# Two ends of a one-core transformer block: the opening dummy matmuls as products of zeros, and the last output block in two column halves

## The chip, the cores and the metric

The kernel runs on one core of one Trainium2 chip. The metric is the device time of one execution in microseconds (us), given as the median of several runs. Five engines take part: TensorE (PE in the profile; its weight loads are a track of their own, PEld), VectorE (DVE), ScalarE (ACT), GpSimd (POOL) and SyncE (SP), which here issues all DMA transfers.

## The reference, cut to what matters

```python
# attention: 2 x 8 heads, 768 tokens, head size 64
q_bits = (q @ proj > 0); k_bits = (k @ proj > 0)          # 6 bits each, a bucket number
scores = where(q_bucket == k_bucket, q @ k.T / 8, -1e9)
a = softmax(scores) @ v                                    # -> x, 2 x 768 x 512
# token and channel mixing
theta = x @ w_theta
u = x + w_tok_r @ (x * cos(theta)) + w_tok_i @ (x * sin(theta))
u = u + relu(u @ w_ch)
# the last layer: 512 -> 2048 -> 512
out = u + relu(layer_norm(u) * g_ln @ w_ch1) @ w_ch2       # 1536 rows of 512 columns
```

## The kernel before, in words

All operands are 32-bit floats. Most matrix products are made of three TensorE instructions each: an operand is split into a rounded high part (`hi`, `hh`, ...) and a remainder (`lo`, `hl`, ...), and high x high, high x low and low x high are added up in PSUM. The order of instructions on every engine is written out by hand: the strings of operation names (`head`, `tail`, `half1`, `trans`, `odd`, `even`, `last`) are walked through from left to right, and each engine executes its own instructions in that order.

**The opening.** Six loads are issued on SP: the first head pair's keys in two halves, the first quarter of the projection (`pbr`), the queries in two halves, and a small table. GpSimd writes a 128x128 identity (`make_identity`), a constant, zeros into `pb_lo` (512 columns), and zeros into two key tiles. `warm(16)` is placed last before the string `head`: it issues 16 TensorE transpositions of the identity into PSUM bank T0, whose result nobody reads. They keep TensorE at work while the first loads are on their way. The string `head` then starts with the splitting of keys and queries (`sh` on ScalarE, `sl` on VectorE), the splitting of the projection (`pb`: `pb_hi` by ScalarE and VectorE, the left 64 columns of `pb_lo` by ScalarE), and the first products: `ac.0` to `ac.3` (the bits of half the keys, the other half, half the queries, the other half; two matmuls of 384 columns each, line 286; `ac.0` writes into the same bank T0 as the dummies), `D.0.0` and `D.0.1` (the first two row blocks of scores, six matmuls each, line 503), `Q.0.0` and `Q.0.1` (the bucket terms added to them, line 515), and `warm.17`, 17 more transpositions of the identity. On VectorE the order is `lok` for two halves, `loq` for two halves (lines 221, 101), four comparisons `bb` (line 310), and the row maxima `M` (line 340); on ScalarE the exponentials `E` (line 356) follow the maxima.

**The end.** The last layer runs in rounds: a round takes 256 of the 2048 hidden columns (a group `g`) and half of the rows (768, six blocks of 128). `o_mm(r, t)` makes the second product of round `r` for row block `t`: six matmuls of 512 output columns into one PSUM bank (T0 and O in turn). `o_add(r, t)` adds the bank to the row block's running sum `U` on VectorE, and in the last group stores the finished block with one DMA of 128 rows of 2 KB. After the last round five such blocks follow each other; block 5 is the last work of the kernel.

Of the kernel before, what the change touches and what calls it, by code (L numbers as in the profile page):

```python
# [9 lines left out]
F32 = mybir.dt.float32  # L10
# [23 lines left out]
def attn_moe_kernel(  # L34
# [28 lines left out]
    vec, act, pool, pe, sp = nc.vector, nc.scalar, nc.gpsimd, nc.tensor, nc.sync  # L63

    def f(ap):
        return ap.bitcast(F32)

    const = ctx.enter_context(tc.tile_pool(name="const", bufs=1))
    psum = ctx.enter_context(tc.tile_pool(name="psum", bufs=1, space=PSUM))

    def bank(tag, name):
        return psum.tile([128, 512], F32, tag=tag, name=name)
# [77 lines left out]
    pb_lo = bp.tile([128, NP, 128], F32R, name="pb_lo")  # L150
# [4 lines left out]
    def r_new(j, dt, name):  # L155
        return const.tile([128, 2, 512], dt, tag=f"R{j}", name=name)
# [4 lines left out]
    def load_raw(n, place=None, which=(0, 1)):  # L161
        b, j = divmod(n, NP)
        for x in which:
            nm, src = (("k", kT), ("q", qT))[x]
            t = place[:, x, :] if place is not None else raw_new(nm, n)
            sp.dma_start(out=t, in_=src[b, 2 * j:2 * j + 2].rearrange("e d s -> (e d) s"))
            raw[nm, n] = t
# [322 lines left out]
    def warm(n):  # L490
        ps = bank("T0", "warm")
        for x in range(n):
            pe.transpose(ps[:, 0:128], ident, ident)  # L493
# [48 lines left out]
    sp.dma_start(out=cst_sb, in_=cst)  # L542
    load_raw(1)
    sp.dma_start(out=pbr[:, 1:NP], in_=pb[:, 1:NP])
    make_identity(nc, ident)
    pool.memset(halfpi, math.pi / 2)
    pool.memset(f(pb_lo), 0.0)
    for t in kz:
        pool.memset(f(t[64:128]), 0.0)
    warm(16)  # L550
    TS = tuple(range(22, 46, 3))
    bg, bg2, bg3 = {}, {}, {}

# [29 lines left out]
    for i in range(8):  # L583
        c, x = divmod(i, 2)
# [74 lines left out]
    def bp_(x, e):  # L659
# [21 lines left out]
        n=s_norm, U=p_transpose, H=p_hi, L=p_lo, PV=pv_mm, O=pv_evac_a, X=pv_evac_b,  # L681
# [48 lines left out]
    def U(i):  # L730
        if i not in U_AT:
            return U0[:, i if i < 4 else i - 2, :]
        j, y = U_AT[i]
        if j not in ur:
            ur[j] = r_new(j, F32, f"u{j}")
        return ur[j][:, y, :]
# [251 lines left out]
    W1, W2 = {}, {}  # L988
# [135 lines left out]
    h_t, ps_t, sn_t, c_t, o_t = {}, {}, {}, {}, {}  # L1124
# [44 lines left out]
        hh, hlo = h_t[r, c]  # L1169
        vec.scalar_tensor_tensor(out=hlo, in0=c_t.pop((r, c)), scalar=0.0, in1=f(hh), op0=ALU.max, op1=ALU.subtract)  # L1170

    def o_mm(r, t):
        g, s = rounds[r]
        e, i = divmod(t, TB)
        ps = o_t[r, t] = bank(("T0", "O")[t % 2], f"o{r}{t}")
        k = 0
        for x in range(2):
            hh, hlo = h_t[r, 10 * (x + 1) + e + 1]
            for lt, y in ((hh, 0), (hh, 1), (hlo, 0)):
                pe.matmul(ps, lt[:, i * 128:(i + 1) * 128], W2[g][:, y, x, :], start=(k == 0), stop=(k == 5))  # L1180
                k += 1

    def o_add(r, t):
        g, s = rounds[r]
        c = ORD[6 * s + t]
        u = U(c)
        vec.tensor_tensor(out=u, in0=o_t.pop((r, t)), in1=u, op=ALU.add)  # L1187
        if g == NG - 1:
            sp.dma_start(out=out[c * 128:(c + 1) * 128, :], in_=u)


    ops.update(
# [2 lines left out]
        ch_br=ch_br, ch_bs=ch_bs, ln_a=ln_a, ln_b=ln_b, ln_c=ln_c, xb_new=xb_new, xn=xn_make, xb_t=xb_t, xb_e=xb_e,  # L1195
        xb_a=xb_a, xb_h=xb_h, xb_l=xb_l, ld=cv_ld, cv_y=cv_y, cv_s=cv_s, cv_b=cv_b, cv_p=cv_p, cv_j=cv_j, cv_h=cv_h, cv_l=cv_l, w1_s=w1_s,
        w1_h=w1_h, w1_l=w1_l, prod=prod, snap=snap, h_add=h_add, h_hi=h_hi, h_lo=h_lo, o_mm=o_mm, o_add=o_add,
    )

    def run(text, **names):  # L1200
        for w in text.format(**names).split():
            op, *args = w.split(".")
            ops[op](*(int(x) if x.isdigit() else x for x in args))
# [204 lines left out]
    for r in range(3, len(rounds)):  # L1408
        g = rounds[r][0] + r % 2
        n = g + 1  # L1410
        a, b, c, d = (
            (f" ld.v.{n}.0 ld.v.{n}.1", f" cv_y.v.{n}.0 cv_s.v.{n}.0.1", f" cv_p.v.{n}.0", f" cv_j.v.{n}.0") if n < NG else ("", "", "", "")
        )
        run(last if g == NG else odd if r % 2 else even, r=r, p=r - 1, g=g, a=a, b=b, c=c, d=d)
    r = len(rounds) - 1
    run("o_mm.{r}.0 h_add.{r}.12 h_hi.{r}.12 o_add.{r}.0 h_lo.{r}.12", r=r)
    for t in range(1, 6):
        run("o_mm.{r}.{t} o_add.{r}.{t}", r=r, t=t)
    order.close()
    zctx.close()  # L1420

# [49 lines left out]
```

## Time and profile before

| | |
|---|---|
| three runs | 665.45, 670.51, 664.65 us (median 665.45) |
| profiled execution | 665.16 us, of which the span from first to last instruction is 663.4 us |
| outside the span | 665.16 - 663.4 = 1.76 us |
| TensorE busy | 657.4 us, 3769 matmuls |

A timeline row gives start and duration of an instruction, or of several alike in a row (x2, x6), counted from the start of the span; what stands behind is engine, line, operation, output <- inputs, form, and in brackets how long the engine had been idle and what released it. A matmul's duration holds its way through the array, so that matmuls in a row overlap; their pace is read from the distance of their starts. The granted TensorE clock is a column of the views by stretch. It reads 1.00 from the first microsecond on in this trace, also where the matmuls' pace is half of the later one; in the opening the level is therefore read from the pace.

### The profile page before, as it was taken

The page shows a single profiled execution, that of the slowest core. Times are in us where ns is not written, and L with a number is a line of the kernel's source. Part 1 is how long each engine was busy: PE and PEld are TensorE (multiplying, and loading weights), DVE is VectorE, ACT ScalarE, POOL GpSimd, SP SyncE. Part 2 cuts the span into 40 slices and gives each one's busy share as a digit, 9 for nine tenths or more (in the row PEclk, how much of TensorE's full clock was granted, in tenths as well). Part 3 has the DMA queues.
Part 4 walks back from the last instruction along what each step waited for, and adds up shares of the span by engine and source line. Part 5 has one row for each costly group of instructions (what it writes and reads, how often), then busy time and mean ns, then how long its engine had stood idle before and what let it go on. Part 6 is the DMA issues. An engine that isn't in the chain of part 4 may idle for free.

```text
span 663.4 us, 11202 instructions
## 1 busy us (share of the span) xinstructions
PE 657.4 (99%) x3769; PEld 591.7 (89%) x3769; DVE 556.9 (84%) x999; ACT 416.7 (63%) x864; POOL 310.4 (47%) x419
## 2 busy tenths in 40 slices
PE   9999999999999999999999999999999999999997
PEld 7999999999999888888888888989998999999996
DVE  6999998999999999999888889986767686867654
ACT  6899998999999886776435534553333433333321
POOL 5887887667787644233433133434150505051400
PEclk9999999999999999999999999999999999999999
DMA  8977544575530411222422122101112121311022
GB/s 247 241 172 171 142 106 114 126 165 124 132 91 1 160 54 57 81 77 98 144 81 64 48 96 68 60 1 64 64 65 75 53 96 34 105 53 33 0 80 111
DMA packets 32230, 62.24 MB, mean 94 GB/s; under 512 B 4466, under 2 KB 11460, under 8 KB 32173
## 3 DMA queue, kind: packets, MB, share of 16 engines
q1 hardware_dynamic: 32173, 61.53, 32.6%
q8 instruction: 30, 0.49, 0.3%
q14 instruction: 27, 0.22, 0.1%
HBM read 39.98 MB, written 3.15 MB: 65 GB/s over the span
## 4 chain that ended last, share of the span: by engine, by line
PE 96%; DVE 2%; DMA 1%; issue 0%; ACT 0%; SPq 0%; POOL 0%; POOLq 0%
PE o L1180 20%; PE acc L853 15%; PE o L405 10%; PE s L332 10%; PE t L380 9%; PE Z L1145 8%; PE a L895 5%; PE v L1145 5%; PE th L787 3%; PE zy L1145 2%; PE Y L1145 2%; PE bits L286 2%; PE s L503 1%; PE warm L493 1%; PE ut L880 1%; PE xt L964 1%
## 5 line engine op out<-in xcount | busy, mean ns | idle before, releaser
L1180 PE MATMUL o<-arena,hh 128*128 128x512 f32 x384 | 118.9, 391 | 0.0
L367 POOL TENSOR_SCALAR pn<-p,l,M 128x768 f32<-128x768 f32 x96 | 94.7, 986 | 38.6 <-DVE l L363 25.8
L340 DVE TENSOR_REDUCE M<-s 128x1 f32<-128x772 f32 x96 | 91.0, 949 | 3.6 <-PE s L515 2.2
L101 DVE TENSOR_TENSOR ptl<-t,pth 128x512 fp32r<-128x512 f32 x144 | 90.6, 680 | 1.5 <-ACT pth L389 1.3
L356 ACT ACTIVATE p<-s,M 128x772 f32<-128x772 f32 x96 | 87.6, 912 | 2.7 <-DVE M L340 2.2
L117 POOL TENSOR_SCALAR cs<-st 128x512 f32<-128x512 f32 (+2 forms) x68 | 44.7, 663 | 84.1 <-DVE cy L131 75.1
L1180 PEld LDWEIGHTS o<-arena,hh 128*128 128x128 f32 x384 | 71.5, 188 | 13.7
L389 ACT ACTIVATE pth<-t 128x512 fp32r<-128x512 f32 x144 | 81.1, 599 | 3.9 <-PE t L380 2.5
L332 PE MATMUL s<-tk,tq 128*128 128x386 f32 (+1 forms) x360 | 82.8, 351 | 0.0
L380 PE MATMUL t<-ident,pn 128*128 128x128 f32 x576 | 80.1, 273 | 0.0
L853 PE MATMUL acc<-arena,tokh 128*128 128x512 f32 x240 | 75.3, 395 | 0.0
L1180 PE MATMUL o<-arena,hl 128*128 128x512 f32 x192 | 75.2, 392 | 0.0
L380 PEld LDWEIGHTS t<-ident,pn 128*128 128x128 f32 x576 | 68.5, 141 | 5.7 <-POOL pn L367 0.6
L1153 ACT ACTIVATE sn<-Z 128x384 f32<-128x384 f32 x39 | 19.2, 492 | 67.2 <-PE Z L1145 67.2
L332 PEld LDWEIGHTS s<-tk,tq 128*128 128x128 f32 (+1 forms) x360 | 59.4, 190 | 0.1
L853 PEld LDWEIGHTS acc<-arena,tokh 128*128 128x128 f32 x240 | 44.0, 188 | 8.5
L1187 DVE TENSOR_TENSOR U<-o,U 128x512 f32<-128x512 f32 x48 | 32.9, 689 | 21.3 <-PE o L1180 20.5
L853 PE MATMUL acc<-arena,tokl 128*128 128x512 f32 x120 | 46.9, 391 | 0.0
L405 PE MATMUL o<-pth,vv 128*128 128x256 f32 x288 | 45.9, 295 | 0.1
L114 ACT ACTIVATE cy<-st 128x512 f32<-128x512 f32 (+2 forms) x72 | 39.6, 562 | 8.1 <-DVE tokl L101 2.5
L131 DVE SCALAR_TENSOR_TENSOR cy<-cy,cs 128x512 uint32<-128x512 uint32 (+2 forms) x72 | 41.4, 575 | 3.6
L125 DVE SCALAR_TENSOR_TENSOR cs<-st,cs 128x512 uint32<-128x512 uint32 (+2 forms) x76 | 44.0, 579 | 0.2
(257 smaller groups left out, 1482.8 us busy)
## 6 DMA issues: line engine op xcount, KB each, us to landing
st<-in_w_dram SPq DMA_DIRECT2D x36, 256.0 KB
st<-in_w_dram SPq DMA_DIRECT2D x14, 512.0 KB
tk<-hik SPq DMA_DIRECT2D x30, 193.0 KB
tq<-hiq SPq DMA_DIRECT2D x30, 192.0 KB
st<-in_wrT_dram SPq DMA_DIRECT2D x12, 384.0 KB
st<-in_wiT_dram SPq DMA_DIRECT2D x12, 384.0 KB
vs<-in_v_dram SPq DMA_DIRECT2D x8, 384.0 KB
tk<-lok SPq DMA_DIRECT2D x15, 193.0 KB
```

What stands on the lines that cost most here:

```text
L101: eng.tensor_tensor(out=o, in0=i, in1=f(hi), op=ALU.subtract)
L117: eng.tensor_scalar(out=s, in0=f(t)[:, :, 1], scalar1=0.0, scalar2=1.0, op0=ALU.mult, op1=ALU.mult)
L332: pe.matmul(ps[:, hf, 0:HW], lt[0:K, x * 128:(x + 1) * 128], rt[0:K, hf, :], start=(K == 128), stop=(K != 128),)
L340: vec.tensor_reduce(out=m_t[p][:, 0, i:i + 1], in_=s_ps[p, i][:, :, 0:HW], axis=AX.XY, op=ALU.max, negate=True)
L356: act.activation(pt, ps[:, :, 0:HW], AF.Exp, bias=m[:, 0, i:i + 1], accum_out=l_t[p][:, 0, i:i + 1])
L367: pool.tensor_scalar(out=pn.rearrange("p (h c) s -> p h (c s)", h=2), in0=p_t.pop((p, i))[:, :, 0:HALF], scalar1=l_t[p][:, 1, i:i + 1], sc ...
L380: pe.transpose(ps[:, w * 128:(w + 1) * 128], pn_t[p, i][:, c, :], ident)
L389: act.activation(ph, t_ps[p, u], AF.Copy)
L405: pe.matmul(ps, vv[:, c, e].rearrange("p a d -> p (a d)"), x[:, c::NI, :], start=(k == 0), stop=(k == 2 * NI - 1),)
L853: pe.matmul(acc, w[:, x, t * 128:(t + 1) * 128], z[:, x, y, :], start=(j == 0 and k == 0), stop=(j == NI - 1 and k == 5),)
L1145: pe.matmul(ps_t[r, b], W1[g][y][:, w, d, :], XB[s][x][:, z, d, :], start=(first == 1 and k == 0), stop=(k == 5), skip_group_check=True,)
L1180: pe.matmul(ps, lt[:, i * 128:(i + 1) * 128], W2[g][:, y, x, :], start=(k == 0), stop=(k == 5))
```

## The change

Two places are changed. In the opening, VectorE writes zeros into the second quarter of `pb_lo` (128 columns) as its first instruction; 38 matmuls of that quarter with itself, 128 columns each, into bank T0 take the place of the 16 transpositions of the identity; VectorE then clears the other three quarters, and GpSimd's clearing of `pb_lo` is gone. The 17 transpositions later in `head` stay. At the end, block 5 of the last round is computed in two halves of 256 columns: six matmuls into bank O, addition and store of the left half, then six matmuls into bank S0, addition and store of the right half.

```diff
@@ opening @@
     load_raw(1)
     sp.dma_start(out=pbr[:, 1:NP], in_=pb[:, 1:NP])
+    vec.memset(f(pb_lo[:, 1]), 0.0)
+    ps = bank("T0", "warm")[:, 0:128]
+    for x in range(38):
+        pe.matmul(ps, pb_lo[:, 1], pb_lo[:, 1], start=True, stop=True)
+    for n in (0, 2, 3):
+        vec.memset(f(pb_lo[:, n]), 0.0)
     make_identity(nc, ident)
     pool.memset(halfpi, math.pi / 2)
-    pool.memset(f(pb_lo), 0.0)
     for t in kz:
         pool.memset(f(t[64:128]), 0.0)
-    warm(16)
@@ end @@
+    def cols(x):
+        return slice(0, 512) if x is None else slice(256 * x, 256 * x + 256)
+
-    def o_mm(r, t):
+    def o_mm(r, t, x0=None, tag=None):
...
-        ps = o_t[r, t] = bank(("T0", "O")[t % 2], f"o{r}{t}")
+        n = cols(x0)
+        if tag == "S0":
+            ps = psum.tile([128, 2, 512], F32, tag=tag, name=f"o{r}{t}")[:, 0, n]
+        else:
+            ps = bank(tag or ("T0", "O")[t % 2], f"o{r}{t}")[:, n]
+        o_t[r, t] = ps
...
-                pe.matmul(ps, lt[:, i * 128:(i + 1) * 128], W2[g][:, y, x, :], start=(k == 0), stop=(k == 5))
+                pe.matmul(ps, lt[:, i * 128:(i + 1) * 128], W2[g][:, y, x, n], start=(k == 0), stop=(k == 5))
...
-    def o_add(r, t):
+    def o_add(r, t, x0=None):
...
-        u = U(c)
+        u = U(c)[:, cols(x0)]
...
-            sp.dma_start(out=out[c * 128:(c + 1) * 128, :], in_=u)
+            sp.dma_start(out=out[c * 128:(c + 1) * 128, cols(x0)], in_=u)
...
-    for t in range(1, 6):
+    for t in range(1, 5):
         run("o_mm.{r}.{t} o_add.{r}.{t}", r=r, t=t)
+    for x, tag in ((0, "O"), (1, "S0")):
+        run("o_mm.{r}.5.{x}.{tag} o_add.{r}.5.{x}", r=r, x=x, tag=tag)
```

TensorE's first instructions before (in brackets the semaphores waited for; `PE_49` is TensorE's own, here the end of the dummies):

```order
L493 MATMUL warm<-ident 128x128 [waits Pool_49]
L493 MATMUL warm<-ident 128x128 x15
L286 MATMUL bits<-hik_80,pb_hi 128x384 [waits DVE_49,PE_49]
L286 MATMUL bits<-lok_81,pb_lo 128x384 [waits Activation_49]
L286 MATMUL bits<-hiq_82,pb_hi 128x384 [waits Activation_49]
L286 MATMUL bits<-loq_83,pb_lo 128x384 [waits DVE_49]
L503 MATMUL s_0_168<-hik_80,hiq_82 128x386 [waits Pool_49]
```

The same place after:

```order
L548 MATMUL warm<-pb_lo 128x128 [waits DVE_49]
L548 MATMUL warm<-pb_lo 128x128 x37
L286 MATMUL bits<-hik_80,pb_hi 128x384 [waits DVE_49,PE_49]
L286 MATMUL bits<-lok_81,pb_lo 128x384 [waits Activation_49]
L286 MATMUL bits<-hiq_82,pb_hi 128x384 [waits Activation_49]
L286 MATMUL bits<-loq_83,pb_lo 128x384 [waits DVE_49]
L503 MATMUL s_0_193<-hik_80,hiq_82 128x386 [waits Pool_49]
```

The dummies now wait for VectorE instead of GpSimd; the first product of the bits still waits for the last dummy's end, and everything behind it stands as before.

TensorE's last block before, and the VectorE additions of the last two blocks before:

```order
L1180 MATMUL o155_7970<-arena_3946,hh1215_7928 128x512 [waits DVE_49]
L1180 MATMUL o155_7970<-arena_3946,hh1215_7928 128x512
L1180 MATMUL o155_7970<-arena_3946,hl1215_7929 128x512
L1180 MATMUL o155_7970<-arena_3946,hh2215_7890 128x512 x2
L1180 MATMUL o155_7970<-arena_3946,hl2215_7891 128x512
```

```order
L1187 TENSOR_TENSOR u_4426<-o_7961,u_4426 128x512 [waits PE_49]
L1187 TENSOR_TENSOR u_4426<-o_7970,u_4426 128x512 [waits PE_49]
```

The same places after:

```order
L1192 MATMUL o155_7995<-arena_3971,hh1215_7953 128x256 [waits DVE_49]
L1192 MATMUL o155_7995<-arena_3971,hh1215_7953 128x256
L1192 MATMUL o155_7995<-arena_3971,hl1215_7954 128x256
L1192 MATMUL o155_7995<-arena_3971,hh2215_7915 128x256 x2
L1192 MATMUL o155_7995<-arena_3971,hl2215_7916 128x256
L1192 MATMUL o155_8004<-arena_3971,hh1215_7953 128x256 x2
L1192 MATMUL o155_8004<-arena_3971,hl1215_7954 128x256
L1192 MATMUL o155_8004<-arena_3971,hh2215_7915 128x256 x2
L1192 MATMUL o155_8004<-arena_3971,hl2215_7916 128x256
```

```order
L1199 TENSOR_TENSOR u_4451<-o_7986,u_4451 128x512 [waits PE_49]
L1199 TENSOR_TENSOR u_4451<-o_7995,u_4451 128x256 [waits PE_49]
L1199 TENSOR_TENSOR u_4451<-o_8004,u_4451 128x256 [waits PE_49]
```

Six matmuls became twelve of half the columns, with the same weights loaded twice; the second six wait for nothing. The last addition became two of half the width, and each is followed by its own store on SP.

## Rows read from the trace of the kernel before

**Rows 1.** The page: busy time of each engine, and the chain that ended last.
```profile
PE 657.4 (99%) x3769; PEld 591.7 (89%) x3769; DVE 556.9 (84%) x999; ACT 416.7 (63%) x864; POOL 310.4 (47%) x419
...
PE 96%; DVE 2%; DMA 1%; issue 0%; ACT 0%; SPq 0%; POOL 0%; POOLq 0%
```

**Rows 2.** Timeline of all engines, 0 to 24 us: dummies, bits, first scores.
```profile
0.71 0.20 POOL masks.py:197 MEMSET ident<- 128x128 f32 x1 [0.29 <-POOLq L1461]
...
0.99 0.29 POOL masks.py:199 TENSOR_SCALAR_AFFINE_SELECT ident<-ident 128x128 f32<-128x128 f32 x1
...
1.26 0.53 POOL L547 MEMSET pb_lo<- 128x512 f32 x1
...
1.34 3.67 PE L493 MATMUL warm<-ident 128*128 128x128 f32 x16 [1.34 <-POOL ident masks.py:199]
...
4.13 0.22 DVE L101 TENSOR_TENSOR pb_hi<-pbr,pb_hi 128x64 fp32r<-128x64 f32 x1
...
5.07 0.69 PE L286 MATMUL bits<-hik,pb_hi 128*128 128x384 f32 x1
...
5.32 0.56 DVE L221 SCALAR_TENSOR_TENSOR lok<-raws,hik 128x384 fp32r<-128x384 f32 x1 [0.97 <-ACT hik L210]
...
5.56 0.52 PE L286 MATMUL bits<-lok,pb_lo 128*128 128x384 f32 x1
...
5.86 1.05 DVE L101 TENSOR_TENSOR loq<-raws,hiq 128x384 fp32r<-128x384 f32 x2
5.88 0.52 PE L286 MATMUL bits<-hik,pb_hi 128*128 128x384 f32 x1
...
6.84 0.52 PE L286 MATMUL bits<-loq,pb_lo 128*128 128x384 f32 x1
...
7.29 0.64 PE L503 MATMUL s<-hik,hiq 64*128 64x386 f32 x2
...
7.77 0.51 PE L503 MATMUL s<-lok,hiq 64*128 64x386 f32 x2
...
8.13 0.51 PE L503 MATMUL s<-hik,loq 64*128 64x386 f32 x2
...
8.56 0.45 PE L286 MATMUL bits<-hiq,pb_hi 128*128 128x384 f32 x1
...
8.85 0.34 PE L286 MATMUL bits<-loq,pb_lo 128*128 128x384 f32 x1
...
9.12 0.62 PE L503 MATMUL s<-hik,hiq 64*128 64x386 f32 x2
```

**Rows 3.** The same timeline further on: first maxima, exponentials and the later dummies.
```profile
9.75 0.55 DVE L310 SCALAR_TENSOR_TENSOR bb<-bits,by 64x384 f32<-64x384 f32 x1
...
11.03 1.83 DVE L340 TENSOR_REDUCE M<-s 128x1 f32<-128x772 f32 x2 [0.73 <-PE s L515]
...
11.27 2.08 PE L493 MATMUL warm<-ident 128*128 128x128 f32 x17
12.09 0.91 ACT L356 ACTIVATE p<-s,M 128x772 f32<-128x772 f32 x1 [1.14 <-DVE M L340]
...
13.14 0.62 PE L503 MATMUL s<-tkz,hiq 128*128 128x386 f32 x2
```

**Rows 4.** Timeline of PE alone around 103 us: products of 256 columns.
```profile
103.24 0.88 PE L405 MATMUL o<-ptl,vv 128*128 128x256 f32 x6
103.95 0.51 PE L332 MATMUL s<-tk,tq 128*128 128x386 f32 x2
```

**Rows 5.** Timeline of all engines, 645 to 664 us: the last block.
```profile
654.83 5.77 SPq L1189 DMA_DIRECT2D out_dram<-u  x5
...
657.99 0.62 PE L1180 MATMUL o<-arena,hh 128*128 128x512 f32 x2
...
659.12 0.39 PE L1180 MATMUL o<-arena,hl 128*128 128x512 f32 x1
659.55 0.69 DVE L1187 TENSOR_TENSOR u<-o,u 128x512 f32<-128x512 f32 x1 [0.67 <-PE o L1180]
```

**Rows 6.** DVE's groups by form: xcount | busy us, mean ns | idle before.
```profile
L423 DVE TENSOR_TENSOR xT<-o,ot 64x256 f32<-64x256 f32 x48 | 19.8, 413 | 0.9
```

**Rows 7.** By stretch: busy of PE, PEld, DVE, ACT, POOL; clock, DMA share, GB/s.
```profile
661.00:662.00 1.00, 0.00 (x0) 0.00 (x0) 0.00 (x0) 0.00 (x0) 0.00 (x0) 1.00 0.68 262
```

## The prediction

> **What bounds the kernel now.** I read the page first: TensorE is busy for 99% of the span and carries 96% of the chain that ended last [rows 1]. So time is won only where TensorE starts its chain earlier, where its instructions become cheaper, or behind its last instruction. The change touches the first and the last few microseconds; in between TensorE executes the same instructions. I therefore read the timeline of these two stretches.
>
> *Opening.* The dummies start at 1.34, when GpSimd has finished the identity (0.99 + 0.29 = 1.28), and end at 1.34 + 3.67 = 5.01; the first product of the bits follows at 5.07, 0.06 behind [rows 2]. The six products of the bits then start 0.32 us apart (5.56, 5.88), which is 1.2 columns per ns, the 1.2 GHz level; from 7.77 on two products of 386 columns take 0.36 (7.77 to 8.13), 0.18 each, the 2.4 GHz level [rows 2]. The granted-clock column shows 1.00 in all of this, so the level stands in the pace alone. The rise lies at about 7.4.
>
> *End.* The last matmul starts at 659.12 and lasts 0.39; the addition follows from 659.55 to 660.24; SP's issue of the last store ends at 654.83 + 5.77 = 660.60, and its data move between 661 and 662 [rows 5, 7]. From the last matmul's end at 659.51 to the span's end at 663.4 nothing runs beside this chain.
>
> **The change part by part: the opening.** The other engines begin at 0.71 [rows 2]. VectorE has done no clearing in this trace. Its row of 128x64 took 0.22, GpSimd's clearing of a tile of the same 128x128 took 0.20 [rows 2]; I take 0.20, so the quarter is ready at 0.91 and TensorE starts 0.05 later (as 1.28 to 1.34) at 0.96, 0.38 earlier than before. The other three clearings, even at 0.22 each, end by 1.6, long before the product that needs them (5.56). GpSimd loses 0.53 of clearing at 1.26 [rows 2], off the path: worth nothing.
>
> One dummy: a product of 384 columns needs 0.32 at the low level, so 128 columns need 0.107. At the high level six products of 256 columns took 0.71 (103.24 to 103.95), 0.12 each [rows 4]; less 128 columns at 2.4 GHz (0.053) leaves 0.066. No row shows a product of 128 columns with its weight load, so the load may be the longer of the two. Bound from above: 0.12 at the high level, since products of 256 columns hide a load in it [rows 4], and 0.21 at the low one, the pace of the transpositions with weights of the same size (3.67 for 16, less the last one's way through the array) [rows 2]. I take 0.107 and 0.066: the trace's products hide their loads at every width that it shows.
>
> First what the row shows: 0.12 per product of 256 columns, hardly above its columns' 0.107 [rows 4]. The Trainium skill ("TensorE: Matmul & The Clock Gate", section Back-to-back issue gap) speaks against the change here: a stream of load and matmul pairs of 128 columns runs at about 81 ns where the columns alone give 56. With that ratio as an estimate, 0.155 and 0.096 per dummy, the dummies would end a microsecond later and the opening would lose 0.4 instead of gaining; the sum would be 665.1.
>
> When does the clock rise? In the trace it rose 2.3 us after the first product (5.07) and 6.1 after the first transposition (1.34). From 0.96 this gives 3.3 to 7.0; I take the middle, 5.1. The second dummy starts at 0.96 + 0.107 + 0.17 = 1.24 (the first load is not hidden: 5.07 to 5.56 is 0.17 more than 0.32), the last one 36 x 0.107 = 3.85 later at 5.09; it ends 0.31 on (0.107 and the 0.20 by which a bits row, 0.52, exceeds its pace) at 5.40, and the bits start at 5.46, 0.39 later than before. But they then run at the high level: 5.46, 5.75 (8.56 to 8.85 is 0.29), 5.93; the fourth needs `lok` (5.32 + 0.56, and 0.05): after it 6.1 and 6.3; the sixth needs the first `loq`, half of 1.05 after 5.86, so 6.45. The first scores follow 0.27 later (8.85 to 9.12) at 6.72, the third 0.29 + 0.18 later at 7.19; before it started at 7.77 [rows 2]. **Gain 0.58.** Any rise up to about 5.6 gives the same, since `loq` is what ends last; with a rise at 7.0 the third score starts at 7.84, a loss of 0.1.
>
> How much of it reaches the end: the first maximum at 11.03 waits for TensorE (idle 0.73), VectorE's work ahead of it ends at 9.75 + 0.55 = 10.30, so it can start up to 0.73 earlier; the exponential at 12.09 waits for it in turn, and the scores at 13.14 stand directly behind the later dummies (11.27 + 2.08, less the overlap) [rows 3]. So the shift passes. Behind this TensorE is the chain. I take 0.5 of the 0.58, with 0 and 0.6 as ends.
>
> **The end.** The twelve half products start 0.12 apart from 657.99: the last at 659.31, ending about 0.28 on (0.88 for six, less five steps) at 659.59, **0.08 later** than before [rows 4, 5]. The addition of 256 columns: the nearest row, 256 columns out of PSUM, took 0.41 against 0.69 [rows 5, 6]: **0.28 less**. The store: 256 KB kept the DMA engines busy for 0.68 us [rows 7]; 128 KB would be 0.34 less if rows of 1 KB move at the same rate, and nothing less if each row costs the same. I take 0.3. The first half's store is issued some 0.7 us ahead and is out of the way. Sum: 0.08 - 0.28 - 0.30 = **-0.5**, ends -0.2 and -0.55.
>
> **Sum.** 665.16 - 0.5 - 0.5 = 664.16 against the profiled execution, which stands 0.29 below the median of 665.45 and inside the two close runs, 664.65 and 665.45. One per cent is 6.65 us, about what a measurement of this kernel tells from no change; no term comes near it.
>
> **The rivals.** *Dummies paced by their weight loads.* Place: TensorE between 0.96 and the first bits product. Price at the transpositions' paces, 0.21 low and 0.11 high (the later 17 took 2.08) [rows 2, 3]: by 5.1 eighteen steps are done, eighteen more take 1.94, the last ends at 7.27, the bits start at 7.33 and the third score at 7.33 + 1.75 = 9.08, 1.3 later than before. With the end's 0.5 the kernel is slower: 666.0. It turns the sum's sign from about 0.17 per dummy at the low level. For it: no product of 128 columns is in the trace. Against: the 0.12 of 256 columns.
>
> *The zeros do not raise the clock.* Then it rises 2.3 after the bits start at 5.46, at 7.76: all six go at 0.32, the first score at 7.68, the third at 8.16, 0.39 later than before; 665.16 + 0.4 - 0.5 = 665.1. For it: 3.67 of dummies before did not raise the clock at once. Against: those were transpositions, and 2.3 of products did. On this row the Trainium skill ("TensorE: Matmul & The Clock Gate", Part 4: PE-mode transpose) says that transpositions do not count as busy in the same way as matmuls; the trace agrees, with 2.3 against 6.1. By that rule the dummies raise the clock and this rival falls, 664.2; without it, 665.1.
>
> *The opening's gain is swallowed.* Loads or VectorE set a later step, and only the end remains: 664.7.
>
> **How the numbers follow.** Forecast 0.50, weight loads 0.25, zeros 0.15, swallowed 0.10. Likeliest: 664.2, its own range 663.6 to 665.1. The range goes down to 0.6 + 0.55 below 665.16, and 0.6 further for the spread of the runs, 663.4; up to the slower rival and 0.4 of spread, 666.4. All cases lie within 1%: faster 0.01, same 0.97, slower 0.02 (a repeat of the 670.51 alone would not do it).
>
> **What would show it.** In the changed trace: TensorE's first row at about 0.96; 38 dummies ending at 4.6 to 5.4 (beyond 6 the weight loads pace them); bits 0.18 apart instead of 0.32; the third score at about 7.2, the first maximum at about 10.5 instead of 11.03. At the end: twelve starts 0.12 apart, a last addition of 0.41, and 0.5 less from the last full block to the end of the span. I am wrong if the bits start after 6.5, if they still run at 0.32, or if the score's gain is gone at 13 us.

## The result, and the profile after

The changed kernel takes 673.88 us (median of 6 runs, 673.41 to 674.74) against 665.05 for the kernel before: **1.3% slower**, ratio 1.0131 with an interval of 1.0112 to 1.015. 664.2 was predicted, with 663.4 to 666.4 as the range. The profiled execution took 674.74, its span is 673.0, so 9.6 longer than before's 663.4.

The page after, busy time and chain (as in [rows 1]):

```profile
PE 668.0 (99%) x3797; PEld 601.8 (89%) x3797; DVE 557.5 (83%) x1004; ACT 416.8 (62%) x864; POOL 309.8 (46%) x418
...
PE 96%; DVE 2%; DMA 1%; issue 0%; ACT 0%; SPq 0%
```

TensorE still is the chain; its busy time grew by 10.6. VectorE's and ScalarE's hardly moved, so no other engine took over. Where it grew stands in the timeline of all engines, 0 to 20 us (answers to [rows 2, 3]):

```profile
0.81 0.17 DVE L545 MEMSET pb_lo<- 128x128 f32 x1 [0.81 <-PEq L1475]
0.95 0.45 DVE L550 MEMSET pb_lo<- 128x128 f32 x3
...
1.03 8.37 PE L548 MATMUL warm<-pb_lo 128*128 128x128 f32 x38 [1.03 <-DVE pb_lo L545]
...
9.46 0.69 PE L286 MATMUL bits<-hik,pb_hi 128*128 128x384 f32 x1
...
9.95 0.52 PE L286 MATMUL bits<-lok,pb_lo 128*128 128x384 f32 x1
...
12.49 0.84 PE L503 MATMUL s<-lok,hiq 64*128 64x386 f32 x2
...
13.13 0.84 PE L503 MATMUL s<-hik,loq 64*128 64x386 f32 x2
...
18.12 1.83 DVE L340 TENSOR_REDUCE M<-s 128x1 f32<-128x772 f32 x2 [2.10 <-PE s L515]
```

The dummies start at 1.03, as forecast. But 38 of them take 8.37 us: less the last one's way through the array, 0.2135 each. The bits start at 9.46 instead of 5.07, **4.39 late**, and then still go at 0.32 per product (9.95 to the next), the low level. Two score products take 0.64 (12.49 to 13.13) where before they took 0.36. The same view of TensorE alone, further on, shows the low level's end:

```profile
18.65 3.89 PE L493 MATMUL warm<-ident 128*128 128x128 f32 x17
22.19 0.99 PE L503 MATMUL s<-tkz,hiq 128*128 128x386 f32 x2
22.98 0.85 PE L503 MATMUL s<-tk2z,hiq 128*128 128x386 f32 x2
23.63 0.85 PE L503 MATMUL s<-tkz,loq 128*128 128x386 f32 x2
24.40 0.65 PE L515 MATMUL s<-bk,bits 7*128 7x386 f32 x2
24.98 0.62 PE L503 MATMUL s<-tkz,hiq 128*128 128x386 f32 x2
25.44 0.52 PE L503 MATMUL s<-tk2z,hiq 128*128 128x386 f32 x2
25.80 0.52 PE L503 MATMUL s<-tkz,loq 128*128 128x386 f32 x2
```

A pair goes at 0.65 up to 23.63 and at 0.36 from 25.44 (to 25.80): the clock rose at about 24.5, where before it rose at 7.4. The 17 later transpositions took 3.89 instead of the 2.08 of [rows 3]. So there are two losses. The scores that stood at 13.14 [rows 3] start at 22.19, 9.05 late, of which 4.39 are the dummies' length and 4.7 the low pace of what lies between; another microsecond goes until 24.4. From there the shift stays: the last block's first matmul stands at 668.17 instead of 657.99 [rows 5], 10.2 late. The opening's loss goes through the other 640 us undiminished.

The last block, timeline of all engines after:

```profile
668.17 0.40 PE L1192 MATMUL o<-arena,hh 128*128 128x256 f32 x2
...
669.48 0.28 PE L1192 MATMUL o<-arena,hl 128*128 128x256 f32 x1
669.80 0.42 DVE L1199 TENSOR_TENSOR u<-o,u 128x256 f32<-128x256 f32 x1 [0.29 <-PE o L1192]
```

From the block's first matmul to the end of the span it is 673.0 - 668.17 = 4.83, before 663.4 - 657.99 = 5.41 [rows 5]: **0.58 gained**, and 10.2 - 0.6 is the 9.6 by which the span grew.

### The profile page after: what moved, and what is told of

It reads as the page before. It is cut to its first block, busy times and chain, and to the rows that moved or that the text cites. A ratio compares the mean times of both kernels' runs of the same rounds, so it can differ in the third digit from the quotient of the medians.

```text
span 673.0 us, 11264 instructions
## 1 busy us (share of the span) xinstructions
PE 668.0 (99%) x3797; PEld 601.8 (89%) x3797; DVE 557.5 (83%) x1004; ACT 416.8 (62%) x864; POOL 309.8 (46%) x418
## 4 chain that ended last, share of the span: by engine, by line
PE 96%; DVE 2%; DMA 1%; issue 0%; ACT 0%; SPq 0%
PE o L1192 20%; PE acc L857 15%; PE o L405 10%; PE s L332 10%; PE t L380 9%; PE Z L1149 8%; PE a L899 5%; PE v L1149 5%; PE th L791 3%; PE zy L1149 2%; PE bits L286 2%; PE Y L1149 2%; PE s L503 1%; PE warm L548 1%; PE ut L884 1%; PE xt L968 1%
## 5 line engine op out<-in xcount | busy, mean ns | idle before, releaser
L1192 PE MATMUL o<-arena,hh 128*128 128x512 f32 (+1 forms) x388 | 119.2, 388 | 0.0
L1192 PE MATMUL o<-arena,hl 128*128 128x512 f32 (+1 forms) x194 | 75.5, 389 | 0.0
```

Source lines behind the costliest of these rows:

```text
L1192: pe.matmul(ps, lt[:, i * 128:(i + 1) * 128], W2[g][:, y, x, n], start=(k == 0), stop=(k == 5))
```

## The experiments

The theories on the opening were these. **A**: a dummy of 128 columns takes as long as its weight load, 0.2135 at the low level, twice what its columns need; dummies of this kind do not bring the clock up, whatever is in them. **B**: zeros do not bring it up. **C**: only the dummies' length costs. **D**: only transpositions bring it up. "Rise" below is the moment at which the clock goes from the low level to the high one, read from the pace in each trace. The kernels share VectorE's clearing and, unless it is said otherwise, the end of the kernel before. Where dummies multiply other values than zeros, their product is read by nobody either.

**The end alone** (the changed kernel with the opening of before).

```diff
-    vec.memset(f(pb_lo[:, 1]), 0.0)
-    ps = bank("T0", "warm")[:, 0:128]
-    for x in range(38):
...
+    pool.memset(f(pb_lo), 0.0)
...
+    warm(16)
```

> The kernel before with only the last block's two halves; its opening as before. All theories agree: the last block gains about 0.6 us (in the changed kernel the distance from the last full block's first matmul to the end of the span fell from 5.4 to 4.8), so 664.5 against 665.05, and none of the 9 us belongs to it. If the halves cost time, it is over 665.5.

664.77 against 665.09, ratio 0.9996 (0.9987 to 1.0005): not told from no change by the runs. The trace shows the gain where it was looked for. TensorE's timeline:

```profile
657.67 0.40 PE L1188 MATMUL o<-arena,hh 128*128 128x256 f32 x2
```

With a span of 662.5 the last block takes 4.83, the same as in the changed kernel. The end has no part in the loss.

**The opening alone** (the kernel before with the new opening).

> The kernel before with only the new opening (38 products of zeros, VectorE clears); its end as before. Both theories on the clock: about 10 us slower than before, 674.5 to 675.2: 4.4 from the dummies' length, 5.7 from a clock that rises at about 24 us instead of 7. If the end's halves had a part in the loss, it is under 673.

674.24, ratio 1.0129 (1.0114 to 1.0144). The opening is the whole loss, within the spread of the runs. In its trace the later transpositions start at 18.64, and the clock rises at about 22.2, two microseconds earlier than in the changed kernel's trace: the time of the rise varies between executions.

**18 thin dummies of zeros.**

```diff
-    for x in range(38):
+    for x in range(18):
```

> As open_only, but 18 dummies instead of 38, so that they end at about 5.1 us at 0.2135 each, as the transpositions did. Theory A (half-idle array: each dummy's 128 columns take 0.107 of 0.2135 us, so that dummies paced by weight loads do not raise the clock, whatever their data): the clock rises late again (after 17 us), products of the opening at 0.32, 5 to 6 us slower, 670 to 671. Theory B (zeros do not raise it): the same. Theory C (only the dummies' length costs, and the late rise came from something behind it, as the loads or VectorE): rise near 7 us, 665.

670.82, ratio 1.0078 (1.0059 to 1.0096). The dummies now end where the transpositions ended, and 5.7 us stay lost. TensorE's timeline:

```profile
1.03 4.10 PE L548 MATMUL warm<-pb_lo 128*128 128x128 f32 x18 [1.03 <-DVE pb_lo L545]
5.19 0.69 PE L286 MATMUL bits<-hik,pb_hi 128*128 128x384 f32 x1
...
7.83 1.01 PE L503 MATMUL s<-hik,hiq 64*128 64x386 f32 x2
...
14.79 3.89 PE L493 MATMUL warm<-ident 128*128 128x128 f32 x17
18.33 0.86 PE L503 MATMUL s<-tkz,hiq 128*128 128x386 f32 x2
19.03 0.51 PE L503 MATMUL s<-tk2z,hiq 128*128 128x386 f32 x2
```

The bits start at 5.19 instead of 5.07, and the low level lasts until about 18.9. Theory C falls: length is not the whole of it.

**18 thin dummies of other values.**

```diff
+    vec.memset(f(pb_hi[:, 1, 0::2]), 1.375)
+    vec.memset(f(pb_hi[:, 1, 1::2]), -0.75)
...
-        pe.matmul(ps, pb_lo[:, 1], pb_lo[:, 1], start=True, stop=True)
+        pe.matmul(ps, pb_hi[:, 1], pb_hi[:, 1], start=True, stop=True)
```

> As zero128x18, but the 18 dummies multiply a quarter of pb_hi in which VectorE has written 1.375 and -0.75 in turn by column, instead of zeros. Theory A (half-idle array): still late, 670 to 671. Theory B (zeros): the clock rises by about 7 us as before, 664.5 to 665.5.

670.37, ratio 1.0075 (1.006 to 1.0091); rise at about 18.1. The values make no difference, so zeros are not what leaves the clock down here.

**18 dummies of zeros with 256 columns.** One thing is changed against the thin ones: the columns behind each weight load (VectorE therefore clears two quarters first, and the dummies start at 1.17 instead of 1.03).

```diff
-    ps = bank("T0", "warm")[:, 0:128]
+    ps = bank("T0", "warm")[:, 0:256]
...
-        pe.matmul(ps, pb_lo[:, 1], pb_lo[:, 1], start=True, stop=True)
+        pe.matmul(ps, pb_lo[:, 1], pb_lo[:, 1:3], start=True, stop=True)
```

> As zero128x18 (18 dummies of zeros, end of the kernel as before), but each dummy multiplies two quarters of pb_lo: 256 columns behind the same weight load. At the low level 256 columns take 0.2135, so the pace, the number of weight loads and the end at about 5.1 to 5.2 stay; only the array's idle half is filled. Theory A (half-idle array): the clock rises by about 7 us as before; 664.5 to 665.5. Theory B (zeros do not raise it) and theory D (only transpositions raise it): late, about 18 to 19 us, 670 to 671.

665.07 against 664.88, ratio 0.9991 (0.9969 to 1.0013): the loss is gone. TensorE's timeline:

```profile
1.17 3.84 PE L548 MATMUL warm<-pb_lo 128*128 128x256 f32 x18 [1.17 <-DVE pb_lo L545]
5.07 0.44 PE L286 MATMUL bits<-hik,pb_hi 128*128 128x384 f32 x1
5.35 0.34 PE L286 MATMUL bits<-lok,pb_lo 128*128 128x384 f32 x1
```

18 dummies with twice the columns take 3.84, not more than the 4.10 of the thin ones, and the first product behind them already goes at the high level (0.28 to the second, as 8.56 to 8.85 in [rows 2]). Theories B and D fall together: zeros that are no transpositions bring the clock up by 4.4. Twice the columns cost no time at the low level, so the thin dummies were paced by something else than their columns. What it is can be read from starts in narrow windows of the timelines, first the changed kernel's, then this one's:

```profile
1.31 0.63 PE L548 MATMUL warm<-pb_lo 128*128 128x128 f32 x2
1.41 0.55 PEld L548 LDWEIGHTS warm<-pb_lo 128*128 128x128 f32 x2
...
1.76 0.63 PE L548 MATMUL warm<-pb_lo 128*128 128x256 f32 x2
1.77 0.54 PEld L548 LDWEIGHTS warm<-pb_lo 128*128 128x128 f32 x2
```

With 256 columns the next load starts with the product, with 128 columns 0.10 behind it, and the next product another 0.11 later (1.31 + 0.2135): product and load seem to take turns. That the load sets the thin pace is argued from these starts; no run parts it from a product of 128 columns that takes as long as one of 256 by itself.

This profile holds a surprise of its own, by stretch (busy of PE, PEld, DVE, ACT, POOL, granted clock, DMA share, GB/s):

```profile
4.50:11.20 6.70, 6.49 (x32) 4.59 (x31) 5.24 (x10) 5.30 (x11) 3.95 (x6) 1.00 0.99 298
11.30:14.60 3.30, 3.30 (x17) 3.30 (x16) 2.81 (x6) 2.93 (x6) 1.63 (x5) 0.50 0.99 311
14.70:20.00 5.30, 5.30 (x32) 4.33 (x31) 3.57 (x4) 2.92 (x6) 2.26 (x6) 1.00 1.09 208
```

In this execution (666.11) the clock fell once more, from 11.3 to 14.7, behind the opening's short products and 0.4 into the 17 later transpositions, which start at 10.85 here. Its other nine runs lie between 663.99 and 665.68.

**18 dummies of other values with 256 columns** (`pb_hi[:, 1:3]` filled as above).

> As zero256x18, but on 1.375 and -0.75 by column in two quarters of pb_hi. Theories A and B: the clock rises by about 7 us, 664.5 to 665.5. Theory D (only transpositions raise it): late, 670 to 671.

664.77, ratio 0.9998 (0.9987 to 1.0009). The dummies go from 1.18 to 5.39, and the bits from 5.44 at the high level. Values make no difference here either.

**11 dummies of zeros with 384 columns** (`pb_lo[:, 1:4]`).

> 11 dummies of zeros with 384 columns (0.32 each at the low level, ending at about 5.0), end of the kernel as before: weight loads are fewer and wholly hidden. Theory A: rise by about 7 us, 664.3 to 665.5. Theories B and D: late, 670 to 671.

664.97, ratio 1.0 (0.9987 to 1.0012); rise at about 6.6. Width, not the number of loads or the values, parts the products that bring the clock up from those that do not.

**Both parts, with dummies of 256 columns** (the changed kernel with 18 of these).

> The changed kernel with 18 dummies of 256 columns of zeros in place of 38 of 128; the last block in two halves as in the changed kernel. Theory A (idle array half of the time in the thin dummies): the clock rises by about 7 us at the latest, and the end's 0.5 stays: 664.2 to 664.8, not above before. If the halves at the end and the opening together had a cost of their own, it is over 666.

664.78 against 665.12, ratio 1.0002 (0.999 to 1.0015). In its trace the opening does what the prediction hoped for: bits from 5.29 at the high level, the third score at 7.00 where the forecast said 7.19 and the trace before has 7.77 [rows 2].

```profile
5.29 0.44 PE L286 MATMUL bits<-hik,pb_hi 128*128 128x384 f32 x1
...
7.00 0.51 PE L503 MATMUL s<-lok,hiq 64*128 64x386 f32 x2
...
12.40 0.62 PE L503 MATMUL s<-tkz,hiq 128*128 128x386 f32 x2
...
657.76 0.40 PE L1192 MATMUL o<-arena,hh 128*128 128x256 f32 x2
```

The scores of 13.14 [rows 3] start 0.74 earlier too, at 12.40, but the last block only 0.23 earlier (657.76 against 657.99), and not earlier than in the trace of end_only with its old opening (657.67). So the opening's gain is not seen at the end of the kernel; whether it was swallowed on the way is not shown by one trace of each. No version here is shown to be faster than the kernel before (the runs of this one lie between 663.97 and 668.56).

**38 dummies of zeros with 256 columns** (length apart from the clock).

> All 38 dummies of the changed kernel, but of 256 columns; the end as before. It parts the two halves of the loss. Theory A: the clock rises between 4 and 7 us, the dummies then go at 0.12, end at 6.5 to 8, and the products behind them run at the high level: third score 0.8 to 2 us later than before, 665.7 to 667, against 674.2 for 38 thin ones. If length is the cause of most of the loss: over 669.

667.02, ratio 1.0032 (1.0019 to 1.0045). Rise at about 4.6, TensorE's timeline:

```profile
1.17 6.30 PE L548 MATMUL warm<-pb_lo 128*128 128x256 f32 x38 [1.17 <-DVE pb_lo L545]
7.53 0.44 PE L286 MATMUL bits<-hik,pb_hi 128*128 128x384 f32 x1
...
9.23 0.51 PE L503 MATMUL s<-lok,hiq 64*128 64x386 f32 x2
```

The third score is 1.46 late (9.23 against 7.77), and the kernel 1.9 slower. The same number of dummies costs 1.9 with the columns filled and 9.1 without (open_only): the 20 too many are the smaller part, the clock is the larger.

**No dummies at the start** (the kernel before without `warm(16)`).

> The kernel before without the 16 transpositions at the start. If the thin dummies simply do not count, leaving them out is no worse than 18 of them: the bits start at about 4.4 at the low level, the clock rises only some 4 to 6 us after the 17 later transpositions begin, 669 to 671. If thin dummies count for something (or do harm of their own), this kernel differs from 670.4 to 670.8 by over 1.5 us.

669.91, ratio 1.0071 (1.0057 to 1.0086); rise at about 17.4. The 16 transpositions of the kernel before are worth 4.8 us, and 18 thin dummies (670.4 to 670.8) are worth nothing. Whether they are worse than none is not shown: the intervals overlap (1.0059 to 1.0096 for the zeros).

**18 thin dummies, and the 17 later transpositions left out** (`warm.17` taken out of `head`).

> zero128x18 without the 17 later transpositions. Theory A': in the opening's products the array has gaps (first loads not hidden, waits between groups), and it was the 17 transpositions, without gaps, that ended the low stretch at 18 to 24 us. Then the clock rises later still, when the transpositions and products of the first row blocks follow each other densely, after 20 us; 671 to 675. If the products of the opening needed only time, the rise stays at 18 to 19 us or earlier, and leaving the 17 out gains: 669 or less.

671.02, ratio 1.0095 (1.0077 to 1.0113). TensorE's timeline:

```profile
15.95 1.01 PE L503 MATMUL s<-tkz,hiq 128*128 128x386 f32 x2 [1.51 <-ACT p L356]
...
21.21 1.06 PE L380 MATMUL t<-ident,pn 128*128 128x128 f32 x4
22.20 0.65 PE L515 MATMUL s<-bk,bits 7*128 7x386 f32 x2
22.77 1.10 PE L380 MATMUL t<-ident,pn 128*128 128x128 f32 x8
```

Four transpositions at the low pace, eight at the high one behind them: rise at about 22.3, against 18.9 and 18.1 with the 17 in the two runs of 18 thin dummies. This suggests that the 17 ended the low stretch earlier, but these are single executions, and the opening with 38 gave 22.2 and 24.5 in two. In time the 17 make no difference here (671.02 against 670.82); without them TensorE waits 1.51 for ScalarE at 15.95.

**Thin products in place of the 17 later transpositions** (opening of the kernel before).

```diff
+            pe.matmul(ps, pb_hi[:, 0], pb_hi[:, 0], start=True, stop=True)
...
-        pb=split_pb, warm=warm, fk=lambda: fake(bk0), kz=kz_copy,
+        pb=split_pb, warm=thin, fk=lambda: fake(bk0), kz=kz_copy,
```

> The kernel before, but the 17 later transpositions (at 11.3 us, at the high level) are 17 products of 128 columns of pb_hi's first quarter with itself. It measures the thin product at the high level. Theory A (paced by the weight load, half as many columns as time): 0.107 each, as the transpositions' 0.109, not the 0.066 of the prediction; and the array is idle half of the time, so the clock may fall behind them and products at 13 us and later go at 0.32 for some us: 666 to 670. If thin products are harmless once the clock is up: 665 and no fall.

665.37 against 664.86, ratio 1.0016 (0.9997 to 1.0036): no loss in the median, where the expectation under A had 666 to 670. But the mean granted clock, on record for every run, is 0.994, 0.992 and 0.990 in the three longest of the ten (667.77, 669.82 and 671.29 us), and not under 0.996 in any of the 12 runs of the kernel before taken beside them. The profiled execution is the longest, 671.29; it gives the pace at both levels:

```profile
10.72 0.89 PE L498 MATMUL warm<-pb_hi 128*128 128x128 f32 x6
```

They go 0.11 apart at the high level, as the expectation under A had it; ten more follow the seventh, which starts at 11.44, and come to 0.2135 each. By stretch the clock shows 0.50 there:

```profile
10.70:11.40 0.70, 0.70 (x7) 0.69 (x7) 0.70 (x2) 0.00 (x0) 0.70 (x1) 1.00 0.75 246
11.60:13.60 2.00, 2.00 (x12) 2.00 (x11) 1.99 (x5) 2.00 (x5) 0.52 (x4) 0.50 1.05 343
14.00:24.00 10.00, 10.00 (x33) 8.25 (x33) 4.48 (x6) 4.55 (x9) 4.23 (x9) 0.50 1.08 264
```

The clock fell at about 11.5 and stayed down until about 25, where in the profile of zero256x18, with transpositions in this place, it fell at 11.3 and was up again at 14.7. So the thin products need not be what drops it; that they do not bring it back, as they did not in the openings, fits the longer fall, but was not tested by itself.

The start of the same trace has the opening of the kernel before, and another rise:

```profile
1.34 3.57 PE L493 MATMUL warm<-ident 128*128 128x128 f32 x16 [1.34 <-POOL ident masks.py:199]
4.97 0.44 PE L286 MATMUL bits<-hik,pb_hi 128*128 128x384 f32 x1
5.25 0.34 PE L286 MATMUL bits<-lok,pb_lo 128*128 128x384 f32 x1
5.43 0.33 PE L286 MATMUL bits<-hik,pb_hi 128*128 128x384 f32 x1
```

Here the first products already go at the high level, so the clock rose before 5.0, before any product had run; with the same opening it rose at about 6.8 in the trace of end_only and at 7.4 in that of the kernel before. Transpositions alone can bring the clock up.

## Why the prediction was wrong, point by point

- **The bound** was right: TensorE carries the chain. **The passing on** holds for the loss: 9.05 at the scores of 13.14, about 10 from 24.4 on, 10.2 at the last block. For a gain of half a microsecond it is not shown: of 0.74 in the trace of dense_both 0.23 was left, so the rival of the swallowed gain stands open. "No term comes near" one per cent was wrong because the same chain passes a loss on.
- **The start** was right in kind: 0.96 forecast, 1.03 measured; the clearing took 0.17 against 0.20, and VectorE began at 0.81, not 0.71.
- **One dummy, "I take 0.107 and 0.066"**, is the first step that failed. Measured are 0.2135 at the low level and 0.11 at the high one, close to the upper bounds that the prediction named, 0.21 and 0.12. The reason given, that the trace's products hide their loads at every width it shows, was no evidence for 128 columns, since it shows none under 256. At the low level a dummy took as long with 128 columns as with 256. That its load is the reason is argued, as said above: the load ahead of a first product, which nothing hides, costs 0.17 there (5.07 to 5.56, less 0.32) and 0.11 at the high level (8.56 to 8.85, less 0.18), and 0.17 alone is not 0.2135. The Trainium skill ("TensorE: Matmul & The Clock Gate", section LDWEIGHTS (loading the stationary operand)) puts a load of 128 columns at 128 / 1.2, some 107 ns. The starts at the low level agree, with 0.11 from a load to the next product; at the high level product and load together took 0.11, which leaves 107 ns only for a load that is hidden.
- **The rise, "From 0.96 this gives 3.3 to 7.0"**, is the second, and the larger. It rose at 24.5. The forecast took products of 128 columns for work like the trace's wider products or its transpositions, and measured the time from their start, from one trace (the same opening gave a rise before 5.0 in another). Shown by the experiments: with 128 columns the rise came at 18 to 24.5, with zeros and with other values, no earlier than without dummies (17.4); with 256 or 384 columns at 4.4 to 6.6.
- **The rivals.** The one on weight loads had the right pace and the right place, but let the clock rise at 5.1 all the same, and so priced 1.3 instead of 9. The one on zeros had a late clock, for a reason that fell (zeros of 256 columns raise it), and with a rise 2.3 after the first bits, which fell too: the opening's own products did not raise it in 9 us. In the trace before, those 2.3 had 3.67 of transpositions ahead of them. What happened joins the two: the dummies' pace of the one, the late clock of the other, and the width of the dummies as the reason of the late clock.
- **The rule on transpositions.** The rule of the Trainium skill ("TensorE: Matmul & The Clock Gate", Part 4: PE-mode transpose), by which transpositions do not count as busy in the same way as matmuls, was held against the rival. The measurements decide otherwise: without the 16 transpositions the clock rises at 17.4 instead of 7.4, and the kernel is 4.8 slower; in the trace of thin17 it rose during the transpositions, before any product.
- **The end** was right: -0.5 forecast, -0.58 measured; matmuls 0.07 later (1.59 against 1.52 for the block), addition 0.42 for 0.41. The store and its waits gave 0.38 where 0.3 was taken, which puts the sum just past its end of -0.55. In the medians this gain is not clear of no change (end_only).

What stays open is why the width decides. The reason that the expectations gave with theory A was not tested by itself, and it has to reckon with 16 transpositions of 128 columns that went at the same 0.2135 and did raise the clock. Open too is why the opening's products (bits, scores of 64 rows, bucket terms of 7 rows) did not raise the clock by themselves, nor always hold it: their gaps and their few rows were not told apart. The spread of the runs is in part the clock's, as the three longest of thin17 show, but not all of it: the longest run of the kernel before on record with its clock, 671.45, has a mean of 1.000.

## What to carry to other kernels

Dummies that are to bring TensorE's clock up must be checked in a trace, by the pace of the products behind them, and not counted: here 18 products of 256 columns and 11 of 384 brought it up, and 18 or 38 of 128 columns did not. The dummies' own pace does not tell, since the 16 transpositions had that of the thin products. The moment of the rise is no constant of an opening either: one opening gave three moments in three traces. The chain that TensorE carries here from end to end passed on a loss of ten microseconds in full, so the opening of a long kernel deserves a bound of its own in a forecast, with a clock that does not rise in the opening as one of its ends.

## What the runs showed of the hardware that was not expected

- A 32-bit product of 128 columns with its weight load takes 0.2135 at the low level and 0.11 at the high one; with 256 columns it takes 0.2135 and 0.12. Half the columns save next to nothing.
- Transpositions of the identity raised the clock (rise at 7.4, 6.8 and before 5.0 in three traces with 16 of them, at 17.4 without), and products of zeros did so as well as others (664.97 and 665.07 against 664.77).
- A clock that is up can fall again in the opening with TensorE busy in every microsecond of the profile: 11.3 to 14.7 us in one execution, 11.5 to 25 us in another.
